# Activation-table loads written out, batch 0's turned probabilities copied by ScalarE alone, and a new order of the work

## The chip, the cores and the metric

The kernel runs on one core of one Trainium2 chip. The metric is the device time of one execution in microseconds (us). A core has five engines with an instruction queue each: TensorE (PE in the profile, its weight loads PEld), VectorE (DVE), ScalarE (ACT), GpSimd (POOL) and SyncE (SP, which here issues every DMA). Each queue is executed in order; engines wait for one another by semaphores.

## The reference

Four batches of clustered attention with 8 heads, 768 positions and head size 64, followed by a feed-forward network (FFN) over the 3072 tokens. Everything is float32.

```
q_assign = argmax(q_n . c_n), k_assign = argmax(k_n . c_n)      # nearest of 16 centroids per head
scores   = (q @ k.T) / 8, and -1e9 where q_assign != k_assign
attn     = softmax(scores, axis=-1)
x        = (attn @ v), heads side by side: [3072, 512]
h        = x @ w_in                                             # w_in  [512, 2048]
g        = h * tanh(log(1 + exp(min(h, 20))))                   # "Mish"
out      = g @ w_out                                            # w_out [2048, 512]
```

## The kernel before

A *unit* is 256 query rows of one head: 4 x 8 x 3 = 96 units, each in two halves `a` of 128 rows. Per half, PE computes the scores `s` (two matmuls `s<-A,B`, two `s<-Z,T` that add the cluster mask as 16 more rows of the contraction), DVE takes the negated row maximum `m` (`rowmax`, line 604), and ACT computes `p = exp(s + m)` and the row sum `l` (`expo`, line 617). The tile `s` has two buffers, so the scores of the half after next wait until ACT has read them.

How `p` goes on depends on the batch. In batch 0 (units 0 to 23, "mode 3") the 128x768 probabilities are turned on PE: `turn` transposes three 128x128 blocks at a time into a PSUM tile `q`, and `back_t` copies `q` back to SBUF as `pt`, four copies per unit and 96 in all. The tile `q` (tag "H") has two buffers, so PE's next turn waits for a copy. Which engine copies is decided by a share: `f_pl` = 0.211 gives 20 of the 96 to DVE (line 692) and 76 to ACT (line 694). In the later batches `p` is split into a high and a low float16 part `hl` (`p_hi`, line 661 on ACT; `p_lo`, line 672 on DVE) and turned by a DMA. Then `pv` multiplies by the values, and `pv_scale`, `pv_out`, `x_out` and `x_low` (lines 763 to 802) make the float16 pair `x` of the FFN's input.

The FFN works on 12 blocks of 256 tokens: `m1` (`h<-x,w`, lines 822 to 824, three matmuls for high x high, high x low and low x high), `e_mish` (`u<-h`, line 831, on ACT, function Mish), the split of `u` into `g` on POOL (835) and DVE (843), and `m2` (`O<-w,g`, lines 859 to 861), then `m_out` on ACT and `m_store`. The weights are first unpacked from 64-bit words in `w_abs` (ACT, Prelu, line 256), `w_f32` and `w_or` (DVE, lines 264 and 271), summed for a scale on PE (`gram`, line 286), and split on POOL and DVE.

ACT evaluates exp and Mish from different tables. Before, the kernel names a table only once, at the start (line 86). Where the next function needs the other one, the framework puts an `ACT_TABLE_LOAD` in front of the activation after the order is fixed. There are 80 loads: that first one, 40 ahead of a Mish (shown at line 831) and 39 ahead of an exp (shown at line 617). Where an activation waits for more than one semaphore, the inserted load takes over one of these waits: 42 of the 80 loads carry one.

The order of all the work is a table of numbers, `PLAN`: each operation of each tile has a place, and `Plan.run` issues them by place, with what an operation needs (`pl.after`) first. This one sequence fixes the order in every queue. The order of the FFN's blocks between the attention units, of the DMA issues and of the copies all follow from it.

Of the kernel before, what the change touches and what calls it, by code (L numbers as in the profile page):

```python
# [56 lines left out]
def tile_clustered_attention_mish_ffn(  # L57
# [28 lines left out]
    nc.scalar.preload_act_table_set("natural_log_exp_and_others")  # L86
    pl = Plan()
    st = {}

# [156 lines left out]
    def w_abs(n):  # L246
        pl.after(("w_load", n))

        i, hf = divmod(n, 2)
        for slot in {0, i + 1} - W.keys():
            W[slot] = wp.tile([P, 1024], F32, tag=f"w{slot}", name=f"w{slot}")
            W16[slot] = W[slot].bitcast(F16)
        hi = stage[n].bitcast(F32).rearrange("p (n t) -> p n t", t=2)[:, :, 1]
        nc.scalar.activation(
            W[i + 1][:, hf * 512 : (hf + 1) * 512], hi, AF.Prelu, scale=2.0**-112, alpha=-(2.0**32)
        )
# [567 lines left out]
    def e_mish(j):  # L826
# [3 lines left out]
        st["u", j] = mp.tile([P, 512], F32, tag="u", name=f"u{j}")  # L830
        nc.scalar.activation(st["u", j], st["h", j], AF.Mish, scale=vst[j // 24, "h"])  # L831
# [56 lines left out]
    ('f_pl', 0): 0.211,  # L888
# [40 lines left out]
def places(args, text):  # L929
# [7 lines left out]
    'qk_load': places(spread(range(0, 32)), """  # L937
        2 1 139 140 379 415 625 624 839 838 972 1020 1115 1260 1414 1444 1603 1640 1861 1785 2042 2087 2158 2304 2495
        2448 2630 2687 2790 2881 2980 3091
    """),  # L940
    'cent_norm': places([()], """
        3
    """),
    'cent_log': places([()], """
        4
    """),
    'cent_root': places([()], """
        5
    """),
    'cent_turn': places([()], """  # L950
        6
    """),
# [12 lines left out]
    'assign_put': places(spread((0, 1)), """
        11 42
    """),
    'w_load': places(spread(range(0, 32)), """
        15 14 47 39 12 59 64 122 66 79 129 154 195 194 200 254 101 97 145 78 187 186 259 258 268 267 321 303 356 388 395
        411  # L970
    """),
    'w_abs': places(spread(range(0, 32)), """
        16 17 48 52 13 60 100 123 80 81 130 155 196 197 201 255 114 115 146 147 188 189 260 261 269 270 322 323 357 389
        396 412
    """),
    'prep_sc': places(spread(range(0, 32)), """
        18 28 142 149 484 562 710 719 870 983 973 1193 1116 1346 1415 1445 1605 1641 1980 2033 2132 2088 2159 2456 2555
        2636 2668 2786 2990 2963 2981 3092
    """),
    'prep_hi': places(spread(range(0, 32)), """  # L980
        19 29 143 312 485 563 711 773 871 984 1108 1194 1308 1423 1548 1642 1742 1826 1981 2051 2133 2260 2359 2457 2556
        2637 2763 2872 2991 3079 3151 3267
    """),
    'copy_t': places(spread(range(0, 32)), """
        20 68 207 313 487 566 743 775 936 1025 1109 1216 1333 1426 1566 1645 1758 1844 1983 2054 2166 2263 2390 2459
        2558 2638 2765 2875 2993 3100 3152 3270
    """),
    'rows_t': places(spread((0, 1)), """
        21 75
    """),  # L990
    'prep_lo': places(spread(range(0, 32)), """
        22 30 198 329 486 564 712 774 890 1006 1140 1223 1311 1424 1564 1643 1743 1842 1982 2052 2154 2261 2387 2458
        2557 2658 2764 2873 2992 3080 3188 3268
    """),
    'w_f32': places(spread(range(0, 32)), """
        23 44 49 53 56 61 112 215 98 82 131 221 224 227 230 271 127 116 212 256 250 244 276 339 319 324 350 353 358 392
        397 413
    """),
    'w_or': places(spread(range(0, 32)), """
        24 45 50 54 57 62 113 216 99 83 132 222 225 228 231 272 128 117 213 257 251 245 277 340 320 325 351 354 359 393  # L1000
        398 414
    """),
    'copy_z': places(spread(range(0, 32)), """
        25 73 199 330 519 565 713 857 935 1024 1141 1224 1378 1425 1565 1644 1757 1843 1998 2053 2186 2262 2401 2483
        2581 2659 2830 2874 3012 3081 3201 3269
    """),
    'rows_z': places(spread((0, 1)), """
        26 74
    """),
    'hot_copy': places(spread(range(0, 32)), """  # L1010
        31 76 293 426 550 567 766 900 1014 1026 1142 1225 1379 1427 1567 1646 1759 1845 2003 2055 2232 2310 2402 2484
        2582 2743 2864 2876 3034 3156 3202 3271
    """),
    'copy_b': places(spread(range(0, 32)), """
        32 148 208 427 520 667 744 858 937 1063 1192 1288 1435 1504 1649 1752 1786 1896 1999 2099 2187 2264 2426 2518
        2654 2744 2831 2925 3013 3101 3223 3353
    """),
    'copy_a': places(spread(range(0, 32)), """
        33 84 294 428 488 649 767 776 1015 1066 1187 1285 1334 1517 1629 1657 1808 1904 1984 2094 2167 2281 2391 2460
        2559 2745 2766 2932 2994 3134 3189 3288  # L1020
    """),
    'scores': places(spread(range(0, 96), (0, 1)), """
# [9 lines left out]
    """),  # L1032
    'rowmax': places(spread(range(0, 96), (0, 1)), """
# [9 lines left out]
    """),  # L1043
    'expo': places(spread(range(0, 96), (0, 1)), """
# [165 lines left out]
    """),  # L1210
    'w_all': places(spread((0, 1)), """
        490 664
    """),
    'w_scale': places(spread((0, 1)), """
        491 665
# [93 lines left out]
```

## Time and profile before

| | us |
|---|---|
| median of three runs | 931.67 (931.4 to 932.89) |
| the profiled execution, its own time | 929.21 |
| span of that execution (first to last instruction) | 927.4 |
| mean granted TensorE clock | 0.994 of full |

The span is what the rows below divide up; 1.8 us of the execution lie around it. "Busy" is the time in which an engine runs at least one instruction, and "idle" the rest. A row `X <- Y` of a list of waits says that engine X sat idle until Y released it; only idle time of the engine that sets the end costs anything.

### The profile page before, as it was taken

Reading aid. Unit: us, or ns where it says so; the run is one execution under the profiler, and the core shown is the slowest. Engines: PE = TensorE matmul, PEld = TensorE weight load, DVE = VectorE, ACT = ScalarE, POOL = GpSimd, SP = SyncE. Lnnn points to the kernel's source line nnn. Section 1 sums busy time; section 2 is a strip of 40 time slices with the busy share of each in tenths; the row PEclk is TensorE's granted clock in tenths of the full one; section 3 lists DMA queues with packets and bytes.
Section 4 is the critical chain, followed back from the end, with each engine's and each line's share of the span. In section 5 each row is a group of like instructions: output and inputs, shape, how many; then the busy total and the mean of one; then the engine's idle time right before and its main releaser. Section 6 shows DMA issues by size and latency. Waiting matters only on the chain. (4 is left out here: it accounts for less than half of the span.)

```text
span 927.4 us, 16133 instructions
## 1 busy us (share of the span) xinstructions
PE 856.8 (92%) x6055; PEld 604.7 (65%) x6055; DVE 624.7 (67%) x1101; ACT 674.7 (73%) x1096; POOL 211.5 (23%) x323
## 2 busy tenths in 40 slices
PE   3588999789999999989999999999999999999998
PEld 3466666557667666577767675676676675776663
DVE  6698897897676777876766778876777767411010
ACT  3666766789799898879999888878898996521120
POOL 2020552422122232211122122123221320211020
PEclk9989999999999999999999999999999999999999
DMA  7668243146747785786776766974777757400000
GB/s 273 248 206 266 58 120 95 30 109 125 135 94 163 151 180 92 160 186 128 134 147 128 131 141 135 185 133 90 123 128 150 149 115 136 80 16 21 13 12 23
DMA packets 252397, 116.18 MB, mean 125 GB/s; under 512 B 230624, under 2 KB 232544, under 8 KB 252320
## 3 DMA queue, kind: packets, MB, share of 16 engines
q1 hardware_dynamic: 252320, 115.15, 57.5%
q8 instruction: 48, 0.79, 0.3%
q14 instruction: 29, 0.24, 0.1%
HBM read 35.68 MB, written 6.29 MB: 45 GB/s over the span
## 5 line engine op out<-in xcount | busy, mean ns | idle before, releaser
L822 PE MATMUL h<-x,w 128*128 128x256 f16 x768 | 209.8, 273 | 3.9 <-ACT u L831 3.9
L824 PE MATMUL h<-x,w 128*128 128x256 f16 x768 | 209.3, 273 | 0.0
L823 PE MATMUL h<-x,w 128*128 128x256 f16 x768 | 209.3, 273 | 0.0
L617 ACT ACTIVATE p<-s,m 128x768 f32<-128x768 f32 x192 | 172.5, 900 | 40.4 <-DVE m L604 29.5
L604 DVE TENSOR_REDUCE m<-s 128x1 f32<-128x768 f32 x192 | 179.9, 949 | 21.2 <-PE s L594 20.0
L672 DVE SCALAR_TENSOR_TENSOR hl<-p,l,hl 128x768 f16<-128x768 f32 x142 | 144.7, 1029 | 49.4 <-ACT hl L661 46.4
L859 PE MATMUL O<-w,g 128*128 128x512 f16 x384 | 146.1, 381 | 1.9 <-ACT osb L867 1.9
L861 PE MATMUL O<-w,g 128*128 128x512 f16 x384 | 145.5, 379 | 0.0
L860 PE MATMUL O<-w,g 128*128 128x512 f16 x384 | 145.5, 379 | 0.0
L661 ACT ACTIVATE hl<-p,l 128x768 f16<-128x768 f32 x142 | 129.9, 929 | 16.1 <-ACT p L617 7.0
L843 DVE SCALAR_TENSOR_TENSOR g<-u,mscg,g 128x512 f16<-128x512 f32 x96 | 75.0, 793 | 97.2 <-POOL g L835 96.9
L589 PE MATMUL s<-A,B 128*128 128x384 f32 x384 | 119.5, 393 | 21.4 <-ACT p L617 15.8
L835 POOL TENSOR_SCALAR g<-u,mscg 128x512 f16<-128x512 f32 x96 | 72.5, 759 | 215.9 <-ACT u L831 151.3
L831 ACT ACTIVATE u<-h,msch 128x512 f32<-128x512 f32 x96 | 63.9, 685 | 61.1 <-DVE g L843 29.8
L594 PE MATMUL s<-Z,T 80*128 80x384 f32 x384 | 101.7, 347 | 0.0
L589 PEld LDWEIGHTS s<-A,B 128*128 128x128 f32 x384 | 63.2, 195 | 48.0 <-ACT p L617 32.7
L822 PEld LDWEIGHTS <-w 128*128 128x128 f16 x768 | 75.1, 98 | 21.4 <-issue 10.5
L823 PEld LDWEIGHTS <-w 128*128 128x128 f16 x768 | 75.2, 98 | 15.2 <-issue 4.4
L824 PEld LDWEIGHTS <-w 128*128 128x128 f16 x768 | 75.1, 98 | 8.6
L629 POOL TENSOR_SCALAR l<-l 128x1 f32<-128x1 f32 x90 | 23.8, 264 | 222.4 <-ACT p L617 207.2
L594 PEld LDWEIGHTS s<-Z,T 80*128 80x128 f32 x384 | 72.3, 195 | 0.0
L859 PEld LDWEIGHTS <-g 128*128 128x128 f16 x384 | 37.5, 98 | 45.7 <-issue 8.3
(201 smaller groups left out, 1173.2 us busy)
## 6 DMA issues: line engine op xcount, KB each, us to landing
qk<-in_qk_dram SPq DMA_DIRECT2D x32, 384.0 KB, 3.9
stage<-in_w_in_dram SPq DMA_DIRECT2D x16, 512.0 KB, 8.2
stage<-in_w_out_dram SPq DMA_DIRECT2D x16, 512.0 KB, 5.2
vraw<-in_vP_dram SPq DMA_DIRECT2D x16, 384.0 KB, 4.1
out_dram<-osb SPq DMA_DIRECT2D x24, 256.0 KB, 2.8
A<-A SPq DMA_DIRECT2D x27, 192.0 KB, 3.1
Z<-B SPq DMA_DIRECT2D x18, 192.0 KB, 3.4
B<-T SPq DMA_DIRECT2D x18, 192.0 KB, 3.2
```

Source lines behind the costliest of these rows:

```text
L589: nc.tensor.matmul(s[:, j, :384], st["B", n][:, q0 : q0 + P], st["A", n][:, j * 384 : (j + 1) * 384], start=True, stop=False,)
L594: nc.tensor.matmul(s[:, j, :384], st["T", n][: D + NCL, q0 : q0 + P], st["Z", n][: D + NCL, j * 384 : (j + 1) * 384], start=False, stop=True,)
L604: nc.vector.tensor_reduce(m, st["s", i, a][:, :, :384], axis=AX.XY, op=ALU.max, negate=True)
L617: nc.scalar.activation(p.rearrange("p (n x) -> p n x", n=2), st["s", i, a][:, :, :384], AF.Exp, bias=st["m", i, a], scale=1.0, accum_out=l,)
L661: nc.scalar.activation(t[:, 0], p, AF.Copy, scale=r)
L672: nc.vector.scalar_tensor_tensor(t[:, 1], p, r, t[:, 0], op0=ALU.mult, op1=ALU.subtract)
L822: nc.tensor.matmul(o, wh, xh, start=(c == 0), stop=False)
L823: nc.tensor.matmul(o, wh, xl, start=False, stop=False)
L824: nc.tensor.matmul(o, wl, xh, start=False, stop=(c == 3))
L859: nc.tensor.matmul(o, gh, wh, start=(f == 0 and fi == 0), stop=False)
L860: nc.tensor.matmul(o, gh, wl, start=False, stop=False)
L861: nc.tensor.matmul(o, gl, wh, start=False, stop=(f == 7 and fi == 1))
```

## The change

Three things change.

The function `table(name)` issues an `ACT_TABLE_LOAD` when the table in use is another one. It is called in `w_abs`, `expo` and `e_mish`, ahead of the activation; a load issued in this way carries no wait of its own. The number of loads stays 80.

`f_pl` becomes 0, so all 96 copies `back_t` of batch 0 run on ACT and none on DVE.

Every list of `PLAN` is replaced. All engines keep the same instructions apart from the 20 copies, in another order. The first FFN tile stands in PE's queue behind the same 640 rows of work as before, and `expo` of 55 halves is ahead of the first Mish in ACT's queue in both. In SP's queue at the start the first of 32 pieces of weights now goes ahead of the first head's `qk`.

```
+    EXPS, MISH = "natural_log_exp_and_others", "mish"
+
+    def table(name):
+        if st.get("table") != name:
+            nc.scalar.preload_act_table_set(name)
+            st["table"] = name
+
+    table(EXPS)
...
     def w_abs(n):
...
         hi = stage[n].bitcast(F32).rearrange("p (n t) -> p n t", t=2)[:, :, 1]
+        table(EXPS)
         nc.scalar.activation(
...
     def expo(i, a):
...
             l = sm.tile([P, 1], F32, tag="l", name=f"l{i}_{a}", bufs=8)
+        table(EXPS)
         nc.scalar.activation(
...
     def e_mish(j):
...
         st["u", j] = mp.tile([P, 512], F32, tag="u", name=f"u{j}")
+        table(MISH)
         nc.scalar.activation(st["u", j], st["h", j], AF.Mish, scale=vst[j // 24, "h"])
...
-    ('f_pl', 0): 0.211,
+    ('f_pl', 0): 0,
...
     'w_load': places(spread(range(0, 32)), """
-        15 14 47 39 12 59 64 122 66 79 129 154 195 194 200 254 101 97 145 78 187 186 259 258 268 267 321 303 356 388 395
+        3 9 18 16 13 14 49 61 19 52 83 97 135 163 210 243 59 60 95 37 141 134 204 266 268 259 335 314 338 358 381 383
...
```

DVE's queue in the first microseconds, before. `Dm0`, `D0` and `onehot0` find the clusters of head 0, `B_0`, `Z_0` are its score operands, `w1` is a piece of weights, `m0_0` is the first row maximum.

```order
L526 TENSOR_REDUCE Dm0_201<-as0_193 128x12
L527 TENSOR_TENSOR D0_200<-as0_193,Dm0_201 128x192
L537 TENSOR_TENSOR D0_200<-D0_200,desc_112 128x192
L538 TENSOR_REDUCE Dm0_201<-D0_200 128x12
L540 TENSOR_TENSOR onehot0_154<-D0_200,Dm0_201 128x12x16
L428 SCALAR_TENSOR_TENSOR B_0_229<-qk0_172,scq_151,A_0_223 128x768
L264 TENSOR_SCALAR w1_220<-w1_220 128x512
L271 SCALAR_TENSOR_TENSOR w1_220<-stage0_218,w1_220 128x512
L436 CAST Z_0_233<-B_0_229 64x768
L557 CAST Z_0_233<-oh0_207 16x3x128 x2
L436 CAST B_0_229<-T_0_225 64x768
L604 TENSOR_REDUCE m0_0_256<-s0_0_251 128x1
```

And now, from the same place in the queue:

```order
L436 SCALAR_TENSOR_TENSOR B_0_217<-qk0_177,scq_151,A_0_179 128x768
L444 CAST Z_0_219<-B_0_217 64x768
L272 TENSOR_SCALAR w1_196<-w1_196 128x512
L279 SCALAR_TENSOR_TENSOR w1_196<-stage0_175,w1_196 128x512
L534 TENSOR_REDUCE Dm0_231<-as0_223 128x12
L535 TENSOR_TENSOR D0_230<-as0_223,Dm0_231 128x192
L545 TENSOR_TENSOR D0_230<-D0_230,desc_112 128x192
L546 TENSOR_REDUCE Dm0_231<-D0_230 128x12
L548 TENSOR_TENSOR onehot0_154<-D0_230,Dm0_231 128x12x16
L565 CAST Z_0_219<-oh0_237 16x3x128 x2
L272 TENSOR_SCALAR w3_209<-w3_209 128x512
L279 SCALAR_TENSOR_TENSOR w3_209<-stage4_201,w3_209 128x512
```

`B_0`, the cast of `Z_0` and one piece of weights have moved ahead of the five cluster steps.

ACT's queue in batch 0, before, from the exp of unit 2 on (`pt1<-q1_0_0` is the copy of unit 1, half 0, part 0, which stands in DVE's queue here):

```order
L617 ACTIVATE p2_0_476,l4_1_477<-s2_0_428,m2_0_433 128x768
L256 ACTIVATE w6_449<-stage11_479 128x512
L694 COPY pt1_492<-q1_0_1_488 128x384
L617 ACTIVATE p2_1_502,l4_1_477<-s2_1_495,m2_1_500 128x768
L617 ACTIVATE p3_0_511,l4_1_477<-s3_0_504,m3_0_509 128x768
L694 COPY pt2_521<-q2_0_0_517 128x384
L694 COPY pt1_492<-q1_1_1_529 128x384
L694 COPY pt1_492<-q1_1_0_534 128x384
```

And now, from the same exp on:

```order
L626 ACTIVATE p2_0_468,l4_1_469<-s2_0_450,m2_0_455 128x768
L703 COPY pt1_479<-q1_0_0_459 128x384
L264 ACTIVATE w10_495<-stage18_379 128x512
L264 ACTIVATE w10_495<-stage19_259 128x512
L264 ACTIVATE w6_457<-stage11_383 128x512
L703 COPY pt1_479<-q1_1_0_510 128x384
L703 COPY pt1_479<-q1_0_1_483 128x384
L626 ACTIVATE p2_1_518,l4_1_469<-s2_1_498,m2_1_516 128x768
L703 COPY pt2_534<-q2_0_0_522 128x384
L703 COPY pt2_534<-q2_0_1_526 128x384
L626 ACTIVATE p3_0_537,l4_1_469<-s3_0_503,m3_0_520 128x768
```

Between the exps of units 2 and 3 there are now five copies where there was one; two of the five (`q1_0_0` and `q2_0_1`) came from DVE's queue.

ACT's queue at the fourth switch to the Mish table and the switch back, before, with the semaphores waited for (`u` is a Mish, `hl` a high part, `xf` a piece of the FFN's input):

```order
L831 ACT_TABLE_LOAD [waits DVE_49]
L831 ACTIVATE u_2662<-h_2636,msch_1416 128x512 [waits PE_49]
L766 ACTIVATE xf_0_0_2671<-o_2530 64x256 [waits Pool_49]
L661 ACTIVATE hl_1_2674<-p_1_2490,l_1_2491 128x768 [waits DMAHW7_49]
L831 ACTIVATE u_2704<-h_2560,msch_1416 128x512 [waits DVE_49,PE_49]
L661 ACTIVATE hl_1_2708<-p_1_2625,l_1_2626 128x768 [waits DMAHW0_49,DVE_49,Activation_49]
L617 ACT_TABLE_LOAD [waits DVE_49]
L617 ACTIVATE p_0_2730,l_0_2731<-s_0_2685,m_0_2690 128x768 [waits Activation_49]
```

And the same place now:

```order
L92 ACT_TABLE_LOAD
L841 ACTIVATE u_2682<-h_2609,msch_1421 128x512 [waits PE_49]
L670 ACTIVATE hl_1_2698<-p_1_2545,l_1_2546 128x768 [waits DMAHW7_49]
L670 ACTIVATE hl_1_2707<-p_1_2659,l_1_2660 128x768 [waits DMAHW0_49,Activation_49]
L841 ACTIVATE u_2727<-h_2497,msch_1421 128x512 [waits PE_49]
L92 ACT_TABLE_LOAD
L626 ACTIVATE p_0_2732,l_0_2733<-s_0_2701,m_0_2730 128x768 [waits DVE_49,Activation_49]
```

The wait for the row maximum (`DVE_49`) has moved from the load to the exp behind it.

## Rows read from the trace of the kernel before

**Rows 1.** The page's first part: busy us (share of the span) xinstructions of each engine.
```profile
PE 856.8 (92%) x6055; PEld 604.7 (65%) x6055; DVE 624.7 (67%) x1101; ACT 674.7 (73%) x1096; POOL 211.5 (23%) x323
```

**Rows 2.** Busy time by stage; columns: stretch, its us, then each engine's busy us.
```profile
0.00:40.00 40.00, 18.53 (x82) 14.98 (x83) 26.34 (x88) 18.75 (x33) 5.86 (x26) 1.00 0.80 289
40.00:208.00 168.00, 143.15 (x1045) 105.57 (x1044) 147.97 (x260) 118.60 (x251) 52.19 (x52) 0.97 0.43 124
208.00:790.00 582.00, 562.44 (x4007) 394.64 (x4006) 425.30 (x718) 507.89 (x767) 134.09 (x216) 1.00 0.72 138
790.00:927.40 137.40, 132.66 (x926) 89.55 (x924) 25.07 (x37) 29.45 (x46) 19.33 (x30) 1.00 0.11 25
```

**Rows 3.** PE's waits from 40 to 208 us: us in total, times, longest.
```profile
PE s L589 <- ACT p L617: 5.1, 6, 2.6
PE q L678 <- ACT pt L694: 3.5, 5, 1.1
...
PE q L678 <- ACT p L617: 2.2, 3, 1.1
PE q L678 <- DVE pt L692: 2.0, 3, 1.1
PE o L725 <- ACT pt L694: 1.7, 2, 1.5
```

**Rows 4.** The table loads, by line and form, whole run.
```profile
L831 ACT ACT_TABLE_LOAD x40 | 51.3, 1283 | 4.1 <-PE h L824 3.5
L617 ACT ACT_TABLE_LOAD x39 | 50.0, 1283 | 16.5 <-DVE m L604 10.4 <-DVE hl L672 5.5
```

**Rows 5.** Five loads that waited, and one activation behind: start us, us, [idle before].
```profile
219.45 1.28 ACT L831 ACT_TABLE_LOAD   x1 [1.32 <-PE h L824]
220.74 1.27 ACT L831 ACTIVATE u<-h,msch 128x512 f32<-128x512 f32 x2
...
241.36 1.28 ACT L617 ACT_TABLE_LOAD   x1 [1.39 <-DVE m L604]
...
353.54 1.28 ACT L831 ACT_TABLE_LOAD   x1 [2.14 <-PE h L824]
...
538.88 1.28 ACT L617 ACT_TABLE_LOAD   x1 [0.47 <-DVE m L604]
...
741.61 1.28 ACT L617 ACT_TABLE_LOAD   x1 [1.25 <-DVE m L604]
```

**Rows 6.** PE's idle gaps within 5.3 us behind those loads.
```profile
221.48 0.27 PE L822 MATMUL h<-x,w 128*128 128x256 f16 x1 [0.71 <-ACT u L831]
...
243.70 0.61 PE L589 MATMUL s<-A,B 128*128 128x384 f32 x2 [0.92 <-ACT p L617]
...
358.75 0.85 PE L465 MATMUL as<-qk,C 128*32 128x384 f32 x8 [0.68 <-ACT p L617]
...
541.22 0.62 PE L589 MATMUL s<-A,B 128*128 128x384 f32 x2 [0.45 <-ACT p L617]
...
743.95 0.62 PE L589 MATMUL s<-A,B 128*128 128x384 f32 x2 [0.78 <-ACT p L617]
```

**Rows 7.** The copies of turned probabilities on ACT and on DVE, whole run.
```profile
L694 ACT COPY pt<-q 128x384 f32<-128x384 f32 x76 | 34.8, 480 | 23.1 <-PE q L678 18.4 <-PE o L725 4.6
L692 DVE COPY pt<-q 128x384 f32<-128x384 f32 x20 | 11.0, 549 | 1.4 <-PE o L725 1.4
```

**Rows 8.** ACT's waits from 40 to 208 us.
```profile
ACT p L617 <- DVE m L604: 11.4, 10, 2.7
```

**Rows 9.** The timeline at the start, DVE and PE.
```profile
11.10 0.36 DVE L526 TENSOR_REDUCE Dm<-as 128x12 f32<-128x192 f32 x1 [3.02 <-PE as L512]
...
12.74 0.36 DVE L540 TENSOR_TENSOR onehot<-D,Dm 128x192 bf16<-128x192 f32 x1
...
13.02 1.01 DVE L428 SCALAR_TENSOR_TENSOR B<-qk,scq,A 128x768 fp32r<-128x768 f32 x1
...
15.12 0.55 DVE L436 CAST Z<-B 64x768 fp32r<-64x768 f32 x1
...
17.88 0.98 PE L589 MATMUL s<-A,B 128*128 128x384 f32 x2 [1.56 <-DVE B L436]
```

More of the change, by code (lines that the diff above doesn't have):

```diff
@@ L84, in tile_clustered_attention_mish_ffn, with table @@
     ps2 = pool("psum2", 2, space=bass.MemoryType.PSUM)
-    nc.scalar.preload_act_table_set("natural_log_exp_and_others")
     pl = Plan()
     st = {}
+    EXPS, MISH = "natural_log_exp_and_others", "mish"
+    def table(name):
+        if st.get("table") != name:
+            nc.scalar.preload_act_table_set(name)
+            st["table"] = name
+    table(EXPS)
     def share(n, key, late):
@@ L255, in w_abs @@
         hi = stage[n].bitcast(F32).rearrange("p (n t) -> p n t", t=2)[:, :, 1]
+        table(EXPS)
         nc.scalar.activation(
@@ L616, in expo @@
             l = sm.tile([P, 1], F32, tag="l", name=f"l{i}_{a}", bufs=8)
+        table(EXPS)
         nc.scalar.activation(
@@ L830, in e_mish @@
         st["u", j] = mp.tile([P, 512], F32, tag="u", name=f"u{j}")
+        table(MISH)
         nc.scalar.activation(st["u", j], st["h", j], AF.Mish, scale=vst[j // 24, "h"])
@@ L936 @@
     """),
[L937 to L940, printed above, removed]
     'cent_norm': places([()], """
-        3
+        1
     """),
     'cent_log': places([()], """
-        4
+        2
+    """),
+    'w_load': places(spread(range(0, 32)), """
+        3 9 18 16 13 14 49 61 19 52 83 97 135 163 210 243 59 60 95 37 141 134 204 266 268 259 335 314 338 358 381 383
@@ new lines @@
+    """),
+    'qk_load': places(spread(range(0, 32)), """
+        4 12 81 90 349 388 611 607 805 700 901 1018 1150 1262 1486 1429 1668 1659 1862 1764 2050 2066 2173 2332 2499
+        2400 2629 2709 2796 2917 3012 3109
+    """),
+    'prep_sc': places(spread(range(0, 32)), """
+        5 32 157 146 455 581 671 699 904 752 1054 1167 1269 1334 1487 1517 1669 1660 1865 1824 2051 2255 2253 2333 2563
+        2633 2758 2869 2971 3074 3159 3200
+    """),
+    'prep_hi': places(spread(range(0, 32)), """
+        6 54 193 322 456 582 672 822 908 1010 1129 1223 1314 1416 1543 1641 1743 1845 1993 2047 2154 2257 2364 2455 2564
+        2634 2759 2870 2972 3075 3160 3265
@@ L946 @@
+    """),
+    'copy_t': places(spread(range(0, 32)), """
+        7 55 194 323 459 584 756 824 923 1041 1130 1234 1329 1417 1566 1643 1755 1850 1994 2048 2164 2279 2413 2469 2565
+        2643 2760 2873 2973 3076 3161 3268
     """),
     'cent_root': places([()], """
-        5
+        8
+    """),
+    'w_abs': places(spread(range(0, 32)), """
+        10 11 47 48 17 39 104 131 51 82 144 175 205 206 234 281 125 127 170 171 214 215 248 295 318 319 362 367 386 409
+        422 448
     """),
@@ L950 @@
     'cent_turn': places([()], """
-        6
+        15
     """),
     'cent_put': places([()], """
-        7
+        20
+    """),
+    'prep_lo': places(spread(range(0, 32)), """
+        21 62 212 346 457 583 673 823 921 1031 1138 1224 1315 1430 1567 1642 1749 1846 1995 2053 2155 2258 2385 2456
+        2571 2635 2772 2871 3000 3095 3201 3266
+    """),
+    'copy_z': places(spread(range(0, 32)), """
+        22 63 213 382 458 603 674 875 922 1073 1154 1233 1378 1431 1571 1661 1754 1870 2010 2068 2184 2259 2393 2465
+        2584 2670 2788 2872 3001 3096 3206 3267
@@ L955 @@
+    """),
+    'w_f32': places(spread(range(0, 32)), """
+        23 70 73 76 34 84 136 174 85 93 160 218 216 221 255 287 154 132 207 261 250 236 297 340 329 341 378 393 420 437
+        424 467
+    """),
+    'w_or': places(spread(range(0, 32)), """
+        24 71 74 77 35 88 137 220 118 94 161 219 235 244 256 288 155 133 208 262 251 254 298 357 330 342 379 394 421 438
+        425 468
     """),
     'assign_mm': places(spread((0, 1)), """
-        8 27
+        25 31
     """),
     'assign_hot': places(spread((0, 1)), """
-        9 40
+        26 64
@@ L961 @@
     """),
     'assign_first': places(spread((0, 1)), """
-        10 41
+        27 65
     """),
     'assign_put': places(spread((0, 1)), """
-        11 42
+        28 66
     """),
[L968 to L986, printed above, removed]
+    'rows_z': places(spread((0, 1)), """
+        29 67
@@ L998 @@
[L998 to L1008, printed above, removed]
+    'copy_b': places(spread(range(0, 32)), """
+        38 164 260 419 525 612 782 895 973 1076 1202 1317 1424 1506 1633 1714 1790 1908 2011 2105 2185 2280 2420 2488
+        2658 2721 2810 2903 3002 3105 3207 3323
@@ L1009 @@
     """),
     'hot_copy': places(spread(range(0, 32)), """
[L1011 to L1016, printed above, removed]
+        40 91 280 399 533 604 757 876 924 1074 1155 1235 1379 1432 1591 1685 1756 1871 2029 2069 2251 2301 2414 2481
@@ L1032 @@
     """),
     'rowmax': places(spread(range(0, 96), (0, 1)), """
[9 rows of a table removed]
[9 rows of a table added]
     """),
     'expo': places(spread(range(0, 96), (0, 1)), """
[9 rows of a table removed]
[9 rows of a table added]
+    """),
+    'p_hi': places(spread(range(0, 96), (0, 1)), """
[9 rows of a table added]
     """),
     'recip': places(spread(range(0, 96), (0, 1)), """
[9 rows of a table removed]
[9 rows of a table added]
+    """),
+    'p_lo': places(spread(range(0, 96), (0, 1)), """
[9 rows of a table added]
+    """),
+    'v_sq': places(spread(range(0, 4), range(0, 4)), """
+        57 100 96 58 440 888 614 751 1121 1180 1539 1670 1919 2090 2308 2525
+    """),
+    'w_sq': places(spread(range(0, 32)), """
+        69 72 75 78 79 89 237 238 239 240 241 242 300 301 302 303 350 351 352 353 354 355 356 368 376 377 380 395 483
+        493 494 495
@@ new lines @@
+    """),
+    'turn': places(spread(range(0, 24), (0, 1), (0, 1)), """
[4 rows of a table added]
+    """),
+    'back_t': places(spread(range(0, 24), (0, 1), (0, 1)), """
[4 rows of a table added]
+    """),
+    'v_sum': places(spread(range(0, 4)), """
+        105 911 1681 2526
+    """),
+    'v_turn': places(spread(range(0, 4)), """
+        106 952 1682 2537
+    """),
+    'v_top': places(spread(range(0, 4)), """
+        107 953 1699 2538
+    """),
+    'v_all': places(spread(range(0, 4)), """
+        108 958 1709 2590
+    """),
+    'v_scale': places(spread(range(0, 4)), """
+        109 959 1710 2591
@@ L1065 @@
+    """),
+    'v_split': places(spread(range(0, 4), range(0, 4)), """
+        115 167 110 113 960 986 1038 1045 1792 1875 1839 1798 2722 2592 2854 2840
+    """),
+    'v_low': places(spread(range(0, 4), range(0, 4)), """
+        116 168 111 114 961 1001 1039 1067 1812 1883 1856 1827 2723 2627 2855 2941
     """),
     'invert': places(spread(range(0, 96), (0, 1)), """
[9 rows of a table removed]
-    """),
-    'w_sq': places(spread(range(0, 32)), """
-        43 46 51 55 58 63 214 217 218 219 220 223 226 229 232 273 314 315 316 317 336 337 338 341 342 343 352 355 360
-        394 477 478
@@ L1080 @@
-    """),
-    'turn': places(spread(range(0, 24), (0, 1), (0, 1)), """
[4 rows of a table removed]
-    """),
-    'p_hi': places(spread(range(0, 96), (0, 1)), """
[9 rows of a table removed]
-    """),
-    'v_load': places(spread(range(0, 4), range(0, 4)), """
-        69 88 86 71 281 703 464 701 1049 1102 1524 1537 1890 1963 2205 2386
-    """),
-    'v_sq': places(spread(range(0, 4), range(0, 4)), """
-        70 89 87 72 302 704 557 702 1072 1162 1545 1672 1919 2063 2265 2521
-    """),
-    'v_sum': places(spread(range(0, 4)), """
-        90 705 1673 2522
@@ L1161 @@
     """),
     'pv': places(spread(range(0, 48), range(0, 3)), """
[7 rows of a table removed]
[7 rows of a table added]
     """),
     'invert_pair': places(spread(range(0, 12)), """
[L1172 removed]
+        229 343 432 534 580 613 741 780 809 894 1052 1068
     """),
[L1174 to L1175 removed]
+    'pv_scale': places(spread(range(0, 96)), """
[5 rows of a table added]
+    """),
+    'pv_out': places(spread(range(0, 96)), """
[5 rows of a table added]
@@ L1203 @@
-    """),
-    'x_low': places(spread(range(0, 96)), """
[5 rows of a table removed]
+        304 601
     """),
     'w_all': places(spread((0, 1)), """
-        490 664
+        507 718
     """),
     'w_scale': places(spread((0, 1)), """
-        491 665
+        508 719
     """),
     'w_hi': places(spread(range(0, 16)), """
-        492 580 582 584 604 634 682 717 763 828 855 916 929 956 967 1011
+        526 574 615 632 634 656 667 733 746 862 867 935 947 966 991 1090
     """),
     'w_lo': places(spread(range(0, 16)), """
-        511 581 583 603 633 640 683 718 764 829 891 917 930 957 1010 1184
+        537 602 616 633 655 666 732 745 795 866 928 946 965 990 1040 1245
```

73 lines of the change are left out of this document (22 added, 51 removed), and 280 rows, old and new, of the table PLAN.

## The prediction

> **What bounds the kernel now.** I read the page's first part, then the busy times by stage, then who PE, ACT and DVE wait for in the stages where PE idles, and last the timeline behind single waits. PE is busy for 856.8 of 927.4 us [rows 1], so it sets the end, and a change is worth what it takes from, or adds to, PE's 70.6 us of idle time. By stage [rows 2], PE idles 40.0 - 18.5 = 21.5 us up to 40 us (nothing is loaded and prepared yet), 168.0 - 143.2 = 24.9 us from 40 to 208 us (attention of batch 0, the first FFN tile at its very end), 582.0 - 562.4 = 19.6 us from 208 to 790 us (attention with FFN work between), and 137.4 - 132.7 = 4.7 us at the end (FFN alone). The two middle stages have different second engines. From 40 to 208 us DVE is at 148.0 / 168.0 = 88% and ACT at 118.6 / 168.0 = 71%; from 208 to 790 us ACT is at 507.9 / 582.0 = 87% and DVE at 73%. The edits go to these two: the copies leave the fuller engine of batch 0, and the loads become cheaper on the fuller engine of the long stage.
>
> **The table loads.** 79 of the 80 loads lie from 208 us on, at 1.283 us each [rows 4]: 51.3 + 50.0 = 101.3 us of ACT, in both kernels, since their number stays. What changes is what they wait for. Before, 42 carry a wait of the activation behind them, and ACT sat idle 4.1 + 16.5 = 20.6 us in front of loads [rows 4]. In the timeline 13 of them have an idle gap of 0.2 us or more ahead, the first at 219.45 us and the last at 741.61 us [rows 5]. Now a load runs while ACT waits for the row maximum or for the FFN's matmuls. So at most 13 x 1.283 = 16.7 us of ACT are saved. PE gains less. Behind five of the 13 loads PE idled on the exp or Mish that followed [rows 6]. Take the load at 241.36 us, which waited 1.39 us for the row maximum [rows 5]: with the load done in that gap, the exp starts 1.28 us earlier, and PE's gap of 0.92 us at 243.70 us closes. In the same way 0.71, 0.68, 0.45 and 0.78 us go (in the fourth case the load waited 0.47 us, which still covers 0.45). At 358.75 us the load is two switches back, but ACT's work from 353.54 us on is unbroken. The sum is 0.71 + 0.92 + 0.68 + 0.45 + 0.78 = 3.54 us. The other eight ended ahead of work that PE did not yet need. Bounds: 0, if the new order puts PE's gaps elsewhere, and -16.7 us; a loss is excluded as to the load itself, which only ever starts earlier in the same queue. I take -3.5.
>
> **The 20 copies.** DVE loses 20 x 0.549 = 11.0 us and ACT gains 20 x 0.480 = 9.6 us [rows 7], all between 40 and 208 us. DVE goes from 148.0 to 137.0 us there, ACT from 118.6 to 128.2, so in sum ACT becomes no fuller than DVE. PE waited 2.0 us on DVE's copies [rows 3]; these three waits go. It waited 5.1 + 2.2 = 7.3 us on exps [rows 3], which stand at the end of a chain scores, maximum (DVE), exp (ACT), and ACT itself waited 11.4 us for maxima [rows 8]. With 11.0 / 148.0 = 7.4% less in DVE's queue I give those 7.3 us 0.5 back. Against that, PE waited 3.5 + 1.7 = 5.2 us on ACT's copies [rows 3]; 9.6 / 118.6 = 8% more in ACT's queue adds 0.4. Sum: -2.0 - 0.5 + 0.4 = -2.1 us. Bounds: -11.0, if all of DVE's relief reaches PE; and +14.4, if none does and each copy holds the exp behind it by its 0.480 us and by the mean wait of ACT's copies for PE's turn, 18.4 / 76 = 0.242 us [rows 7]: 20 x 0.722. I stay near -2, since the two nearest rows are PE's own waits.
>
> Two pages of the Trainium skill pull apart here. TensorEngine Tiling (Array Packing), section PSUM Bottleneck, says to share the emptying of PSUM between ScalarE and VectorE; this change takes VectorE out of it for the turned probabilities, and by that rule the third rival below is right. Perfetto Trace Analysis, section Optimizing Scalar/DVE Operations, says that work of a saturated VectorE may go to ScalarE. The trace stands nearer the second, with 88% against 71% in this stage.
>
> **The new order.** At the start, DVE idled 3.02 us until 11.10 us for PE's cluster scores, and the operand `B` (1.01 us) and the cast of `Z` (0.55 us), which need no clusters, came after them, ahead of PE's first scores at 17.88 us [rows 9]. Now both stand in that gap. That takes 1.56 us out of the path between the last cluster step (12.74 us) and 17.88 us; a piece of weights moves in and one out of it. PE's transposes of the one-hots, which DVE's `B` covered, show instead, so I take 1.0 for it. PE also waits for five pieces of weights ahead of the second scores where it waited for six, for which I add 0.5: -1.5 us. The first head's load now stands behind 512 KB of weights in SP's queue; at the 289 GB/s of this stage [rows 2] that is 1.8 us, hidden as long as head 0's data is there by the time that PE has the centroids. If it isn't, the start is 0.3 us slower. Bounds: -4 and +1.8. For the rest of the order I find no reason of either sign: ahead of the first FFN tile each engine has the same work as before, save the copies. I take 0. Its bounds are what an order can do: it can't win more than the 19.6 us that PE idles in the long stage, nor do I see it lose more; near 0, it is good for some 4 us either way, a fifth of that.
>
> **Sum.** -3.5 - 2.1 - 1.5 = -7.1 us. The profiled execution took 929.2 us (1.8 around its span), 2.5 below the median 931.67 of the runs; against its own time that makes 922.1, and against the median 924.6. I forecast 924.6.
>
> **Rivals.**
> 1. *DVE was the whole bound of batch 0.* Then its 11.0 us come off PE's 24.9 us of idle time in full: 931.7 - 11.0 - 3.5 - 1.5 = 915.7. For it: 88% busy, and ACT's waits for maxima. Against it: of PE's longer waits there, more end on ACT than on DVE [rows 3].
> 2. *No effect.* PE's work is given, the gaps closed behind loads open again at the next wait, and the copies cost ACT what they save DVE: -1.5 to +1.5, thus 930.2 to 933.2. For it: eight of 13 waiting loads had no gap of PE behind them, and 9.6 is close to 11.0. This also covers loads that would still wait, though the order shows them without one.
> 3. *ACT's queue becomes the bound of batch 0: slower.* A copy waits at the head of ACT's queue for PE's turn, with the next exp behind it, and PE's turns wait for the exp. At 0.722 us for each of 20 copies, less the 3.5 and the 1.5 and the 2.0 of DVE's copies: 14.4 - 7.0 = +7.4, so 939. Fewer hits give 934 to 939; it decides from some ten copies on PE's path, where 7.2 us outweigh 7.0. For it: ACT's copies already wait 23.1 us [rows 7], and five copies now stand between two exps where one stood. Against it: 49.4 us of ACT's 168.0 are idle there.
>
> **How the numbers follow.** Forecast (920 to 928) 0.50, rival 1 0.10, rival 2 0.20, rival 3 0.20. This kernel's measurement can tell some 0.2%, 1.9 us: faster is below 929.8, slower above 933.5. Faster has the forecast, rival 1, and 0.06 of rival 2 (with the loads' gain kept in part): 0.66. The same: 0.14. Slower: 0.20. The range leaves out about 0.1 at either side: below, rival 1 near its full price (915); above, the upper half of rival 3: 935. The forecast's own range alone would be 920 to 928.
>
> **What would show it.** Loads: all but a few rows of `ACT_TABLE_LOAD` stand without idle time ahead, and the idle time is ahead of the exp or Mish instead; PE's waits on ACT from the FFN's start on fall by some 3 us. Copies: DVE's share in batch 0 falls to about 82%, the first FFN matmul starts some 3 to 4 us earlier than before, and PE's waits for copies grow by less than 1 us. Start: PE's first scores at about 16.9 us. I am wrong if the first FFN matmul comes no earlier, if PE's idle time after it grows, or if the loads' rows grow longer than 1.283 us where they start early.

## The result and the profile after

The changed kernel takes 908.12 us (median of 4 runs, 907.34 to 909.94), the kernel before 931.53 us in the same session: a ratio of 0.9752, with a 95% interval of 0.9730 to 0.9775, or 23.4 us less. The prediction had 924.6 us, 7.1 less, and a range that ended at 915. The profiled execution has a span of 908.2 us and took 909.94.

The page's first part for the changed kernel, busy us (share of the span) and instructions of each engine:

```profile
PE 853.5 (94%) x6055; PEld 602.9 (66%) x6055; DVE 611.9 (67%) x1081; ACT 678.5 (75%) x1116; POOL 211.0 (23%) x323
```

Against [rows 1], PE has nearly the same work (853.5 for 856.8 us), DVE has lost 12.8 us and ACT has gained 3.8. The two spans differ by 19.2 us, some 4 less than the medians of the runs, since the execution profiled before was 2.3 us faster than its median and this one 1.8 us slower. Of the 19.2, 15.9 are idle time of PE (70.6 us before, 54.7 now), and the rest is some of its work in shorter time. By stage, with the columns of [rows 2]:

```profile
0.00:40.00 40.00, 17.97 (x83) 14.65 (x83) 28.34 (x90) 21.85 (x40) 5.70 (x26) 0.94 0.76 277
40.00:208.00 168.00, 151.26 (x1119) 112.73 (x1120) 142.40 (x247) 131.12 (x279) 55.27 (x56) 0.94 0.51 139
208.00:790.00 582.00, 570.92 (x4093) 401.84 (x4092) 424.35 (x724) 506.83 (x771) 134.67 (x219) 1.00 0.70 137
790.00:908.20 118.20, 113.38 (x763) 73.67 (x761) 16.86 (x23) 18.74 (x29) 15.31 (x23) 1.00 0.06 20
```

In 40 to 208 us PE now does 74 more matmuls, and in 208 to 790 us it idles 11.1 us where it idled 19.6. The first FFN matmul comes at 191.55 us; it came at 201.56. So 10 of the 19.2 us between the two traces are won ahead of the FFN, and 9 behind it.

PE's waits from 40 to 208 us, and the table loads and copies, which answer to [rows 3], [rows 4] and [rows 7]:

```profile
PE q L687 <- ACT pt L703: 8.9, 12, 1.7
PE s L597 <- ACT p L626: 4.6, 6, 2.1
PE q L687 <- ACT p L626: 1.4, 1, 1.4
```

```profile
L92 ACT ACT_TABLE_LOAD x80 | 102.6, 1283 | 2.1 <-PEq L1308 0.7
L703 ACT COPY pt<-q 128x384 f32<-128x384 f32 x96 | 42.9, 482 | 18.8 <-PE q L687 14.9 <-PE o L734 3.6
```

The waits on DVE's copies are gone. The loads last as long as before and no longer stand behind idle time: 2.1 us in front of all 80, where it was 20.6 in front of the 79 of [rows 4].

At the start the prediction's step is seen and its effect is not. `B` and the cast of `Z` now run in DVE's gap, at 8.48 and 9.51 us (13.02 and 15.12 before [rows 9]), but the first scores start at 18.29 us instead of 17.88 (18.3 to 18.5 in all the traces with the new start). ACT's queue ahead of them, before and then now:

```profile
13.89 1.34 ACT L565 ACTIVATE T<-oh,mbi,msc 16x384 fp32r<-16x384 bf16 x2
15.25 0.83 ACT L434 CAST A<-A 64x768 fp32r<-64x768 f32 x1
```

```profile
15.31 1.34 ACT L573 ACTIVATE T<-oh,mbi,msc 16x384 fp32r<-16x384 bf16 x2 [4.43 <-DVE Z L565]
16.67 0.67 ACT L264 ACTIVATE w<-stage 128x512 f32<-128x512 f32 x1
17.36 0.83 ACT L442 CAST A<-A 64x768 fp32r<-64x768 f32 x1
...
18.29 0.98 PE L597 MATMUL s<-A,B 128*128 128x384 f32 x2 [1.57 <-ACT A L442]
```

The last operand cast `A`, which PE now waits for, comes 2.11 us later. One part of that is a piece of weights that stands ahead of it on ACT (0.69 us). The larger part, 1.42 us, is that ACT's copy of the turned one-hots `oh` into `T` now starts only when DVE's copy of them into `Z` has ended (14.09 + 1.12 us); before, DVE made its copy at 15.71 us, after ACT's.

### The profile page after: what moved, and what is told of

Its sections match the earlier page's. It is cut to its first block, busy times and chain, and to the rows that moved or that the text cites. A ratio compares the mean times of both kernels' runs of the same rounds, so it can differ in the third digit from the quotient of the medians.

```text
span 908.2 us, 16108 instructions
## 1 busy us (share of the span) xinstructions
PE 853.5 (94%) x6055; PEld 602.9 (66%) x6055; DVE 611.9 (67%) x1081; ACT 678.5 (75%) x1116; POOL 211.0 (23%) x323
## 5 line engine op out<-in xcount | busy, mean ns | idle before, releaser
L670 ACT ACTIVATE hl<-p,l 128x768 f16<-128x768 f32 x142 | 129.9, 928 | 17.6 <-DVE l L650 9.3
L831 PEld LDWEIGHTS <-w 128*128 128x128 f16 x768 | 75.1, 98 | 22.8 <-issue 11.1
L638 POOL TENSOR_SCALAR l<-l 128x1 f32<-128x1 f32 x90 | 26.6, 295 | 241.6 <-ACT p L626 235.7
```

The source lines that it names most:

```text
L670: nc.scalar.activation(t[:, 0], p, AF.Copy, scale=r)
L831: nc.tensor.matmul(o, wh, xh, start=(c == 0), stop=False)
```

## The experiments

All times are medians; ratios are to the kernel before on the same chip. "FFN" is the start of the first FFN matmul in the profiled execution.

| run | kernel | us | before | ratio, 95% interval | FFN, us |
|---|---|---|---|---|---|
| | the change | 908.12 | 931.53 | 0.9752 (0.9730 to 0.9775) | 191.55 |
| e1 | loads alone | 921.73 | 930.81 | 0.9891 (0.9874 to 0.9908) | 204.66 |
| e2 | order alone | 924.46 | 930.81 | 0.9937 (0.9919 to 0.9954) | 193.68 |
| e3 | order and loads | 913.19 | 930.81 | 0.9807 (0.9792 to 0.9822) | 197.23 |
| e4 | order and copies | 918.09 | 930.81 | 0.9856 (0.9838 to 0.9875) | 188.11 |
| e5 | before, one-hots first | 929.93 | 930.85 | 0.9986 (0.9970 to 1.0002) | 199.12 |
| e6 | new order up to the FFN | 926.14 | 930.85 | 0.9942 (0.9922 to 0.9963) | 193.97 |
| e7 | change, DVE filled up | 912.38 | 930.85 | 0.9800 (0.9777 to 0.9824) | 192.87 |
| e8 | change, `A` on POOL | 909.22 | 930.85 | 0.9764 (0.9739 to 0.9789) | 190.31 |
| e9 | before, scores early | 928.14 | 931.32 | 0.9970 (0.9953 to 0.9987) | 198.86 |
| e10 | new order up to 45 us | 928.17 | 931.32 | 0.9962 (0.9947 to 0.9977) | 197.99 |
| e11 | the change again | 907.53 | 931.32 | 0.9741 (0.9723 to 0.9759) | 187.71 |
| e12 | change, loads ahead | 923.57 | 931.32 | 0.9908 (0.9887 to 0.9929) | 188.36 |
| e13 | change, 3 loads at waits | 905.69 | 933.10 | 0.9706 (0.9682 to 0.9731) | 192.26 |
| e14 | the change again | 909.04 | 933.10 | 0.9746 (0.9722 to 0.9770) | 190.47 |

No run has the copies in the old order: with all of them on ACT, the engines' queues wait for one another in a ring there. So what the copies are worth is known for the new order only.

### e1 to e4: the parts

e1 is the kernel before with the calls of the loads; e2 has the change's table of places and nothing else; e3 is both; e4 is e2 with the copies.

```
e1, e3:  + table(EXPS) / table(MISH)  ahead of each Prelu, Exp and Mish
e2, e3, e4:  PLAN of the change
e4:  - ('f_pl', 0): 0.211,   + ('f_pl', 0): 0,
```

> The kernel before with the table loads called explicitly at their place, in the old order and with the old copies. Theory 'loads' (the load's early start is worth more than the gaps behind five loads, since PE's whole lead over ACT in the FFN stage grows): 919 to 925 us. Theory 'order' (most of the 23 us comes from the new order) and theory 'copies' (DVE bound batch 0, and its relief brings the first 10 us): 926 to 929 us, near the 3.5 us of the prediction's sum, and the first FFN matmul at 201 us as before.

> The new order alone: loads as before (not called), 20 copies of batch 0 still on DVE. Theory 'order': 910 to 917 us, and the first FFN matmul at 191 to 194 us. Theory 'copies': the order is fitted to fewer copies on DVE and is worth little without that, 925 to 933 us, first FFN matmul at 199 to 203 us. Theory 'loads': 926 to 932 us.

> The new order and the explicit loads; 20 copies of batch 0 still on DVE: the change without its copies. Theory 'copies': 917 to 922 us, 9 to 14 us over the changed kernel's 908.1, all of it lost before the first FFN matmul. Theory 'order': 908 to 911 us. Theory 'loads': within 2 us of the changed kernel, and 8 us or more under the run without the explicit loads.

> The new order and all copies of batch 0 on ACT; loads not called: the change without its loads. Theory 'loads': 915 to 920 us. Theory 'order' and theory 'copies': 910 to 912.5 us, i.e. 2 to 4 us over the changed kernel, with the first FFN matmul at 191 to 192 us since no load lies ahead of it.

Each part gains, and what a part gives hardly hangs on the others. The loads give 9.1 us in the old order (930.81 - 921.73), 11.3 in the new one (e2 - e3), and 10.7 beside the copies (e4's 12.7 against the change's 23.4). The order alone gives 6.4. The copies give 6.4 without the loads (e2 - e4) and 5.8 with them (e3's 17.6 against 23.4). (Order, loads and copies taken in this row, 6.4 + 11.3 + 5.8, make up the whole by construction; that the loads give about the same in three settings and the copies in two is what shows that the parts add.) No theory that gives the gain to one part stands: the times of e1 and e4 are as "loads" had them, e2's FFN start is as "order" had it but its time is not, and e3's 913.19 lies between what the three expected. (The changed kernel's 23.4 us were measured in another session than e3's and e4's differences.)

Where the loads' 10 us come from is seen with e1, which keeps before's order on every engine. Its exps, set against the same exps of before, come earlier in steps: nine of 1.23 to 1.28 us, the length of a load, between 223 and 743 us, each behind a load that had waited, and three smaller ones. Between 177 and 743 us e1 goes from 2.9 us behind before (its granted clock was 0.92 from 40 to 208 us, before's 0.97) to 7.4 ahead: 10.4 us. The nine steps make 11.5 us; on balance about 1 of them is given back in between. First the kernel before, at one such load and at PE's next long wait on ACT, and at another such pair:

```profile
565.63 1.28 ACT L617 ACT_TABLE_LOAD   x1 [1.77 <-DVE hl L672]
566.92 0.90 ACT L617 ACTIVATE p<-s,m 128x768 f32<-128x768 f32 x1
...
577.49 0.61 PE L589 MATMUL s<-A,B 128*128 128x384 f32 x2 [1.24 <-ACT p L617]
...
614.05 1.28 ACT L617 ACT_TABLE_LOAD   x1 [1.67 <-DVE hl L672]
...
634.07 0.27 PE L822 MATMUL h<-x,w 128*128 128x256 f16 x1 [1.43 <-ACT u L831]
```

The same places of e1:

```profile
563.10 1.28 ACT L92 ACT_TABLE_LOAD   x1
564.88 0.90 ACT L626 ACTIVATE p<-s,m 128x768 f32<-128x768 f32 x1 [0.49 <-DVE hl L681]
...
575.49 0.62 PE L597 MATMUL s<-A,B 128*128 128x384 f32 x2 [0.34 <-ACT p L626]
...
610.40 1.28 ACT L92 ACT_TABLE_LOAD   x1
612.07 0.90 ACT L626 ACTIVATE p<-s,m 128x768 f32<-128x768 f32 x1 [0.39 <-DVE hl L681]
```

Before, the load waits for DVE's `hl`, and the exp runs behind it at 566.92 us. PE's gap comes 10.6 us behind that exp, at 577.49, and in the second case 20.0 us behind the load, at 634.07, on another activation (a load that waited, at 627.36 us, lies between). In the first case ACT's queue has one break of 0.30 us in between, so it carries the delay to the next place where PE needs ACT. In e1 the first gap has shrunk from 1.24 to 0.34 us, and the second is gone.

Set matmul against matmul, PE itself goes from 3.1 us behind before to 7.5 ahead. At the five gaps of [rows 6] it wins 0.9, 1.2, 0.7, 0.5 and 1.0 us, 4.3 in all. It wins some 6.3 us at other gaps that ended on ACT: 0.5 at 255.59 us, 1.2 at 577.49, 1.5 at 634.07, 1.3 at 681.96 and 686.56, 1.2 at 710.13, 0.6 at 745.38. They lie 2 to 13 us behind the last load that had waited. Four of them, before; in e1 none of the four is left:

```profile
255.59 0.62 PE L589 MATMUL s<-A,B 128*128 128x384 f32 x2 [0.28 <-ACT p L617]
...
681.96 0.27 PE L822 MATMUL h<-x,w 128*128 128x256 f16 x1 [0.73 <-ACT u L831]
...
710.13 0.61 PE L589 MATMUL s<-A,B 128*128 128x384 f32 x2 [0.73 <-ACT p L617]
...
745.38 0.61 PE L589 MATMUL s<-A,B 128*128 128x384 f32 x2 [0.45 <-ACT p L617]
```

PE's waits on ACT from 208 to 790 us, before and then e1:

```profile
PE s L589 <- ACT p L617: 10.7, 15, 1.8
PE h L822 <- ACT u L831: 3.9, 4, 1.4
```

```profile
PE s L597 <- ACT p L626: 5.9, 7, 2.1
PE O L869 <- ACT osb L877: 1.1, 1, 1.1
PE h L831 <- ACT u L841: 1.0, 1, 1.0
```

### e5, e9, e10 and e6: where the order gains

Between the first exp (20.5 us in both) and the fifth, e2 wins 4.5 us on before. Three kernels take this apart: e5 moves one step of the start in the old order, e9 some more, e10 takes the whole new start. e6 has the new order up to the FFN. All four have the loads and the 20 copies as before.

```
e5:  copy_t, copy_z, rows_z, rows_t, hot_copy of head 1: right behind its assign_put
e9:  e5, and copy_a(1), scores(0,1) ahead of w_sq(1); rowmax(0,1), scores(1,0) ahead of v_sum(0);
     turn(0,1,0) ahead of scores(1,1)
e10: new order for places below 142, then the old order
e6:  new order for places below 1116 (the first m1), then the old order
```

> The kernel before with one step moved: the second head's casts of B, Z and T, and its copy, stand on DVE and ACT right behind its one-hots, ahead of five pieces of the weights where they stood behind them. Theory 'pieces' (the order's gain up to 47 us, 4.5 us at the fifth exp, comes from the 5.4 us of pieces that no longer stand ahead of the second scores): the fifth exp starts 2.5 to 4.5 us earlier than before, at 43 to 45 us, and the first FFN matmul some 3 us earlier; 927 to 929 us. Theory 'loads of data' (it comes from the other order of the input DMAs): fifth exp at 47 us as before and 930 to 932 us.

> The kernel before with more of the start moved, beside the one-hots of the run before: the second scores stand ahead of four pieces' Gram products on PE, the third scores ahead of the values' norm, and one turn ahead of the fourth scores, so that the copy behind it no longer holds ACT for 4 us. Theory 'scores first' (the 4.5 us at the fifth exp come from this order of PE and ACT): fifth exp at 43 to 45 us, first FFN matmul 2 to 4 us earlier than before, 927 to 929 us. Theory 'the rest' (input order and the pieces' places make it): fifth exp at 46 to 48 us, 929 to 931 us.

> The new order up to the sixth scores (some 45 us), the old order from there on; loads not called, 20 copies on DVE. Fifth exp at 43 to 43.5 us as in the new order. Theory 'start is half' (the order's 6.4 us are some 3.5 to 4.5 from the start and the rest from batch 0 behind it): 926 to 928 us, first FFN matmul at 197 to 198.5 us. Theory 'start is caught up' (PE has to wait for DVE later anyway): first FFN matmul at 200 us or later, 929 to 931 us.

> The new order up to the first FFN matmul, the old order from there on; loads not called, 20 copies on DVE. Theory 'batch 0' (the order's whole gain is won before the FFN starts and the new order of the long stage is worth nothing): 922 to 926 us, within 2 us of the new order alone (924.5). Theory 'both' (the long stage's new order gives or takes as well): more than 2 us off that, on either side.

e5's theory falls: the fifth exp came at 46.95 us, 0.7 earlier than before's 47.62, and the time is hardly changed. Taking a wait from DVE alone, with PE's and ACT's order kept, did not help. Before, ACT's copy of a turn waits for PE, with the next exps queued behind it:

```profile
40.54 0.48 ACT L694 COPY pt<-q 128x384 f32<-128x384 f32 x1 [3.80 <-PE q L678]
...
42.03 0.91 ACT L617 ACTIVATE p<-s,m 128x768 f32<-128x768 f32 x1
```

In e2 the copies there wait 0.44 us, and the same exp starts at 38.69:

```profile
35.50 0.86 ACT L694 COPY pt<-q 128x384 f32<-128x384 f32 x2 [0.44 <-PE q L678]
...
38.69 0.90 ACT L617 ACTIVATE p<-s,m 128x768 f32<-128x768 f32 x1 [0.53 <-DVE m L604]
```

e9, which brings the turns and scores forward, gains 3.2 us, as much as the whole new start in e10 (3.2). Its time and its FFN start are as "scores first" had them; its fifth exp, at 46.44 us, is not, and e10's, at 45.03, came later than expected too. (In these two traces the first exp already came late, at 22.08 and 21.11 us against 20.53; from there to the fifth e9 wins 2.7 us on before, e10 3.2 and e5 0.9.) So the start is worth some 3 us; which of e9's moves makes it was not taken further apart. The other 3 to 4 us of the order are won from there to the FFN (e6 starts it at 193.97 us, e10 at 197.99), spread over many places. The long stage's new order is worth nothing that can be told: e6 ends 1.7 us above e2, within the intervals of both.

### e7: is it DVE's time that the copies free?

```
  nc.scalar.copy(pt, o)
+ (at the 20 former places of DVE's copies)
+ nc.vector.tensor_reduce(cz, ident three times over, op=max)
```

> The changed kernel with 20 reductions of 128x384 numbers on DVE, some 0.55 us each, at the places of its former copies; ACT makes all copies as in the change, and nothing waits for the reductions. They compute nothing that is used. Theory 'DVE's time' (the copies' 5 to 6 us come from the 11 us taken out of DVE's queue): 912 to 915 us, the gain undone, first FFN matmul at 196 to 198 us. Theory 'the copies' own latency' (the gain is that PE no longer waits for a copy that stands in DVE's queue): 908 to 910 us.

The line of the added work in e7:

```profile
L705 DVE TENSOR_REDUCE cz<-ident 128x1 f32<-128x384 f32 x20 | 10.9, 543 | 0.1
```

It put 10.9 us back into DVE's queue, and e7's ratio is 0.9800 where the change has 0.9746 (the middle of its three): 5.0 us of the copies' 6 are lost again, with some 3 us of uncertainty. The traces lean the same way but can't settle it: from the 13th exp to the first FFN matmul it takes 117.1, 120.4 and 117.0 us in e2, e3 and e6, with copies on DVE, 113.1 us on average (111.3 to 114.6) over the seven traces with the order and ACT's copies, and 116.1 us in e7, so 3.0 of 5.1 us come back there. Single traces differ by as much: e2 and e3, with the same work in the same order up to the FFN, start it at 193.68 and 197.23 us, and e7 at 192.87, earlier than expected. By the medians, then, DVE's time is the larger part, and not the delay of a copy that PE waits for.

### e8: does all of ACT's time count?

```
- ('f_a', 1): 0.0853,   + ('f_a', 1): 0.5,
```

> The changed kernel with 10 more of the operand casts `A` of batches 1 to 3 on POOL instead of ACT (0.93 us each there). Theory 'ACT's queue' (in the long stage what ACT's queue loses comes off the end nearly one for one, as 1.28 us per waiting load did): 898 to 903 us. Theory 'waits only' (only time in front of a wait counts, work in between is hidden): 906 to 910 us. If POOL's 1.05 us per cast delays the scores, 910 to 914 us.

From 190 to 770 us ACT did 503.3 us of work for the change's 513.2, and nothing came of it: 909.22 us, where "waits only" had it, at a ratio within the change's interval. But e8 doesn't test its first theory cleanly. The cast of `T`, which stands behind `A` in ACT's queue, reads `A`, and ACT now sat idle there until POOL had made it. From ACT's waits in this stretch:

```profile
ACT T L446 <- POOL A L426: 6.7, 6, 2.1
```

The change has no such wait there. So 6.7 of the 9.8 us that ACT was spared came back as waits for POOL, and whether work taken off ACT's queue pays back in general stays open. What e1 shows is narrower: the loads that counted stood at the head of ACT's queue behind a wait, with an exp or a Mish behind them.

### e12 and e13: where a load may stand

e12 calls each load right behind the last activation that uses the old table; e13 moves only three, each in front of an instruction at which ACT idled.

```
e12: + ahead()  behind each Prelu, Exp and Mish: loads the table that the next one of them needs
e13: + if calls in (384, 460, 481): table(the other one)   ahead of that ACT instruction
```

> The changed kernel with each table load called right behind the last activation that uses the old table, not right ahead of the next that needs the new one. In the changed kernel's trace ACT idles 5.8 us between such a pair of activations that a load could fill. Theory 'waits on the chain' (a load costs when it stands behind a wait, whichever instruction waits): 903 to 907 us. Theory 'all covered' (the loads that waited for maxima and matmuls are the ones that counted): 907 to 910 us. If the loads delay what stands between, 910 to 914 us.

> The changed kernel with three of its 80 table loads moved ahead, each to stand right in front of an instruction between the two activations where ACT idled in the changed kernel's trace: an `A` cast at 349.0 us (idle 1.12 us), an `xf` at 425.9 (0.46, and 0.76 at the next one), an `xf` at 449.6 (1.95). Theory 'at the wait' (a load is free in front of the instruction that waits, and costs its 1.28 us where ACT has work that others wait for; the 16 us of the run before came from loads put ahead of ready casts): 3 x 1.2 = 3.6 us less at most, 904 to 906.5 us, and never slower than the changed kernel. Theory 'ahead is bad as such' (a load away from the activation that needs it costs, wherever it stands): 909 us or more.

> The changed kernel once more, on the same chip as the next one, as its control: 907 to 910 us.

> The changed kernel as control on the same chip: 907 to 910 us.

e12 is 16.0 us slower than its control e11. Its last condition, "If the loads delay what stands between", had the kind, and none had the size. ACT and DVE around one load, e12 first:

```profile
263.68 1.28 ACT L99 ACT_TABLE_LOAD   x1
264.97 0.94 ACT L684 ACTIVATE hl<-p,l 128x768 f16<-128x768 f32 x1
...
265.95 1.02 DVE L695 SCALAR_TENSOR_TENSOR hl<-p,l,hl 128x768 f16<-128x768 f32 x1 [1.81 <-ACT hl L684]
...
268.10 0.69 ACT L855 ACTIVATE u<-h,msch 128x512 f32<-128x512 f32 x1 [1.61 <-DVE g L868]
```

The same in e11:

```profile
262.16 0.92 ACT L670 ACTIVATE hl<-p,l 128x768 f16<-128x768 f32 x1
...
263.10 1.28 ACT L92 ACT_TABLE_LOAD   x1
263.11 1.02 DVE L681 SCALAR_TENSOR_TENSOR hl<-p,l,hl 128x768 f16<-128x768 f32 x1 [0.38 <-ACT hl L670]
```

In e12 the load stands ahead of a cast `hl` that was ready, and DVE waits 1.81 us for that cast where it waited 0.38. DVE's next work, `g`, comes late, and a Mish waits 1.61 us for it. That is one place of many; the exps of e12 fall behind e11's in some ten steps from 217 us on. e13 is the counter-test: three loads moved just as far, but to places where ACT idled. One of them, in the change and then in e13:

```profile
349.01 0.94 ACT L428 ACTIVATE A<-qk,scq 128x768 fp32r<-128x768 f32 x1 [1.12 <-PE s L597]
...
354.43 1.28 ACT L92 ACT_TABLE_LOAD   x1
```

```profile
348.57 1.28 ACT L92 ACT_TABLE_LOAD   x1
349.87 0.94 ACT L105 ACTIVATE A<-qk,scq 128x768 fp32r<-128x768 f32 x1
```

e13 takes 905.69 us, 3.35 less than e14 on the same chip; expected were up to 3.6. In the traces its exps gain on e14's in three steps, of 1.4, 0.7 and 1.3 us, behind the three places. The intervals of e13 and e14 meet, but the steps stand at the right places. e13 has the lowest ratio of all, though not clear of the noise. That a load away from its activation costs as such is out.

## Why the prediction was wrong

**The loads, -3.5 predicted, some -10 measured** (9.1 to 11.3). This is the largest error, and the step that failed is "Behind five of the 13 loads PE idled on the exp or Mish that followed". The mechanism was right: the 13 waits, the loads running ahead, the bound of 16.7. The five gaps of [rows 6] closed as forecast: they gave 4.3 us in e1 for the 3.5 of the sum. But I looked for PE's loss only there. That "the other eight ended ahead of work that PE did not yet need" failed: the delay stayed in ACT's queue, and PE paid some 6 us for it at other gaps, up to 13 us behind the last load that had waited. Two of these even stood within the 5.3 us of [rows 6] and were not listed: 0.28 us at 255.59, behind the load at 253.25, and 0.45 us at 745.38. Nine of the 13 brought their full length.

**The copies, -2.1 predicted, some -6 measured.** What failed is "I stay near -2, since the two nearest rows are PE's own waits". Those rows name the engine that came last [rows 3]; the time that DVE spent on copies also delayed maxima, and so exps, that stand under ACT's name. From 40 to 190 us ACT's exps waited 12.8 to 14.3 us for maxima in e2, e3 and e6, with copies on DVE, 9.9 to 11.7 us in the seven traces with the order and ACT's copies, and 11.9 us in e7. By its median, e7 gives most of the gain back with idle reductions. The first rival had the right kind (DVE bounds batch 0), with 11.0 us a price too high. The third, ACT's queue, had a true part: PE's waits on ACT's copies rose from 5.2 to 8.9 us (those on all copies from 7.2 to 8.9), where I expected less than 1 us more. But PE's idle time in the stage fell from 24.9 to 16.7 us all the same.

**The start, -1.5 predicted; 0.4 later at the first scores, yet some -3 by the end.** The step "That takes 1.56 us out of the path" failed: the path went over to ACT, where the last cast came 2.11 us later, 1.42 of it behind DVE's copy of the one-hots and 0.69 behind a piece of weights. "a piece of weights moves in and one out of it" counted DVE's pieces alone, and nothing in the sum looked at ACT's queue. The gain came behind the first scores, where I had looked at the order of the weights' pieces only. That the sign came out right is luck.

**The rest of the order, 0 (±4) predicted, some -3 measured**, within its bounds, and ahead of the FFN as far as e6 can tell. "ahead of the first FFN tile each engine has the same work as before" was true and no argument: what changed was what stood behind what.

All four errors go the same way: 6.5 + 3.9 + 1.5 + 3 = 15, close to the 16.3 us between the forecast gain of 7.1 us and the measured 23.4. In this kernel, in which PE idles in many short waits, each counted by itself looked cheaper than it was.

## What to carry to other kernels

A delay in a queue with little slack does not show where it arises; follow the queue to the next places where the bounding engine waits for it, or compare the starts of the same instructions in two traces and look for steps. Call a table load in front of an instruction that waits: three loads moved to such places brought 3.35 us (e13), and loads put right behind the last use of the old table, some of them ahead of work that was ready and that others waited for, cost 16.0 us in all (e12). The name in a row of waits is the engine that came last; it does not tell which engine's load would have to fall.

## What the runs showed of the hardware

TensorE's granted clock fell to half, 1.2 of 2.4 GHz, for some 3 to 10 us between 150 and 190 us in 13 of the 16 traces. In e2 this came behind a stretch in which PE had often waited. Its rows, with the columns of [rows 2]:

```profile
156.00:159.00 3.00, 2.78 (x26) 2.11 (x22) 2.07 (x6) 3.00 (x8) 1.64 (x2) 1.00 0.16 34
159.00:162.00 3.00, 1.39 (x9) 1.39 (x10) 3.00 (x6) 1.92 (x5) 0.00 (x0) 1.00 0.00 0
162.00:165.00 3.00, 1.99 (x9) 1.49 (x8) 2.91 (x5) 2.97 (x7) 1.17 (x2) 0.50 0.54 156
165.00:168.00 3.00, 3.00 (x14) 2.44 (x13) 2.61 (x6) 2.02 (x5) 2.40 (x2) 0.50 0.34 74
168.00:171.00 3.00, 3.00 (x13) 2.90 (x12) 1.75 (x7) 2.40 (x5) 0.91 (x1) 0.50 0.00 0
```

In e4 the same stretch had PE busy for 1.80, 1.29 and 2.67 of 3 us, and the clock stayed at 1.00. From 150 to 190 us the granted clock was 0.87 in all three traces with the new order and DVE's copies, and 0.91 to 1.00 in the seven with ACT's. So up to 40 us x (0.94 on average - 0.87) = 2.8 us, an estimate as if PE had been busy all along, of what the copies gain may reach PE as clock and not as shorter waits; I had not reckoned with it. That it does is not shown. In the old order, with DVE's copies, the clock there was 0.91 to 1.00 as well, and in e7, with DVE filled up, 0.91. The mean clocks of whole executions do not tell the kernels apart: 0.983, 0.984, 0.982 and 0.984 on average for e2, e3, e4 and the change, with up to 0.02 between the runs of one kernel. What sets off the fall in one execution and not in another stays open.
